# A planned kernel whose planner prices an operation by when its successor can begin

## The chip, the cores and the metric

The kernel runs on one core of one Trainium2 chip. The metric is the device time of one execution in microseconds; of several executions the median is given.

## What is computed

Three layers in a row on a batch of 4 sequences of 576 tokens, all in float32:

```
scores = q kT / 8 - slope * (i - j) where 0 <= i - j < 128      # 8 heads of 64
x      = softmax(scores) v                                      # (4, 576, 512)
u      = x + (relu(xT w_tok1) w_tok2)T                          # mixes tokens, hidden 256
u      = u + relu(u w_ch1) w_ch2                                # hidden 1536
out    = u + relu(norm(u) w1) w2                                # hidden 2048, norm with g_ln
```

The weights come in float64 and are brought to float32 on the chip.

## The kernel before

**Tiles.** The 2304 tokens are 18 tiles of 128. Every matmul operand of the three layers behind the attention is split into a high and a low part of the type that the fast matmul takes, and a product is three matmuls: high by high, low by high, high by low. The sums stay in float32 in `u`, one tile of 128x512 for each of the 18.

**Attention stage (about the first 160 us).** For each tile: scores on PE (line 625, two groups of heads), a predicated copy that folds the second key tile into the first (DVE, line 660), bias, scale and row minimum in one instruction per head (DVE, line 666), the exponential with its row sum (ACT, line 675), a transpose on PE into the one PSUM buffer `ps_t` (line 682), a copy of it to SBUF (ACT, `pf`, line 384), two triangular selections on POOL (line 692), values on PE (line 637) into the one PSUM buffer `ps_v`, and a normalization: copy `ut` (ACT), transposes back (PE, line 704), multiplication into `u` (DVE, line 400). The token layer (`tok1`, lines 469 to 471, and `tok2`, lines 764 to 766) is fed in between, three pieces for each half tile (`TOK_RATE`). The weights of that layer are converted in the same stage: a DMA brings the 8-byte numbers into `rh` and `rw` (`rh` has one buffer), ACT makes `e` from `rh` (line 445), DVE makes the float32 number in four instructions (lines 448 to 460).

**Products stage (the rest).** The two channel layers go through 14 steps each for two blocks of eight tiles, and 14 narrow ones for two tiles. In a step, `seven_products` (lines 1125 to 1127) makes a hidden block of two by two parts with seven products in place of eight, ACT and DVE evacuate, and `second` (lines 1238 to 1240) multiplies by the second weight into one of two PSUM buffers `tok`, which DVE adds to `u` (line 1243). The last layer's second block uses `second_fast` (line 1275). Sums and low parts on operands in SBUF may go to DVE or to POOL (`minus`, lines 400 and 402), whichever the planner finds.

**The order.** Each engine works its instructions off in the order of the program, and waits on semaphores where an input is not there. That order comes from a planner, class `Plan`. Every operation is recorded with a cost for each engine that may do it, its reads and its writes. `ranks` gives each a due time: PE operations from the running sum of PE costs, the others later, and then backwards through what depends on them:

```python
late[d] = min(late[d], late[k] - self.lat(e, e2) - self.STRETCH * ops[d][0][e])
```

`order` then plays the program: it goes to the engine that is free first, takes the due-soonest operation that is ready there, and sets

```python
start[k], free[e] = max(at, free[e]), max(at, free[e]) + ops[k][0][e]
...
ready[j] = max(ready[j], free[e] + self.lat(e, "PE" if "PE" in ops[j][0] else "") if k in ops[j][2] else at + 1)
```

So a cost is how long the engine is taken, and a latency `LAT` comes on top of it before a reader on another or the same engine may begin (140 more where the reader is PE). The operations are then emitted in the order of `start`. The times of this play are used for nothing else. With equal times the engine whose name comes first in the alphabet is served first, DVE before POOL. An engine is held for an operation that is due earlier and ready within `HOLD` (200 for DVE and ACT, 300 for POOL).

The costs stand in the functions `dve`, `act`, `pool_tt`, `pool_ts` and `pe` (lines 313 to 334) and as plain numbers at some calls of `op`.

Of the kernel before, what the change touches and what calls it, by code (L numbers as in the profile page):

```python
# [35 lines left out]
HW = CW // 2  # L36
# [84 lines left out]
class Plan:  # L121
# [13 lines left out]
    SPARE = {"DVE": 1200, "ACT": 0}  # L135
    LAT = {"PE": 400, "DVE": 260, "ACT": 290, "POOL": 180, "DMA": 4000, "CTL": 0}

# [175 lines left out]
def dve(n, fast=False):  # L313
    return 150 + n / (1.92 if fast else 0.97)


def act(n, psum=False, pointers=0):
    return 170 + (0.82 if psum else 0.9) * n + 93 * pointers


def pool_tt(n):
    return 150 + 2.4 * n

# [5 lines left out]
def pe(n):  # L329
    return 2.6 + n / 2.4  # L330


def pe2(n):
    return 13 + n / 2.4


def block_kernel(tc, qT, kT, v, wt1, wt2, wa1, wa2, wb1, wb2, g, bias, out):
# [72 lines left out]
    def load_f64(src, k, n, dst=None, get=None):  # L410

        rh = buf("raw", [P, DM, 4], I16, "rh", 1)
        rw = buf("raw", [P, DM, 2], U32, "rw", 2)
        e = buf("cvt", [P, DM], BF16, "e", 1)
        s = buf("cvt", [P, DM], BF16, "s", 1)
        m = buf("cvt", [P, DM], U32, "m", 1)  # L420
        at = k * P * n * 8
        flat = src.bitcast(U8).rearrange("r b -> (r b)")

        def rows(x, first):
            return x.rearrange("p n t -> p (n t)"), flat[first:first + P * n * 8].rearrange("(p b) -> p b", p=P)
# [12 lines left out]
        load_half(rw, at + 3)  # L438

        def half(x):  # L440
            return x.t[:, :n].bitcast(I32)

        op({"ACT": act(n)}, lambda: nc.scalar.activation(  # L445
            out=e.t[:, :n], in_=head(BF16), func=AF.Copy, scale=2.0 ** -116), [rh], [e])

        op({"DVE": 1.3 * dve(n // 2, True)}, lambda: nc.vector.tensor_scalar(
            half(s), half(e), 3, EXP16, ALU.logical_shift_left, ALU.bitwise_and), [e], [s])
        op({"DVE": 1.3 * dve(n // 2)}, lambda: nc.vector.scalar_tensor_tensor(  # L450
            out=half(s), in0=half(e), scalar=SIGN16, in1=half(s), op0=ALU.bitwise_and, op1=ALU.bitwise_or), [e], [s])
        op({"DVE": 1.3 * dve(n, True)}, lambda: nc.vector.tensor_scalar(
            m.t[:, :n], rw.t[:, :n, 0], 4, None, ALU.logical_shift_left), [rw], [m])
# [6 lines left out]
        op({"DVE": 1.3 * dve(n)}, lambda: nc.vector.scalar_tensor_tensor(  # L460
            out=get(), in0=m.t[:, :n], scalar=2.0 ** 32, in1=s.t[:, :n], op0=ALU.add, op1=ALU.mult), [m, s], [dst])
        return dst, get
# [144 lines left out]
    def packed(i, i2):  # L607
# [21 lines left out]
        if i2 is not None:  # L629
            tiles2 = keys_of(i2)[0]  # L630
            na = len(tiles2)
            for c in range(2):
                def values(c=c, pf=pf_t[i2, c]):
                    for p in range(2):
                        for a, kt in enumerate((i2, i2 - 1)[:na]):
                            for j in range(2):
                                nc.tensor.matmul(pv.t[j * D:(j + 1) * D, 2 * c + p], vs[kt].t[:, 4 * c + 2 * p + j],  # L637
                                                 pf.t[:, a, 2 * p + j], start=(a == 0), stop=(a == na - 1))

                parts.append((na * 440, values, [(pf_t[i2, c], a) for a in range(na)] + [vs[kt] for kt in tiles2],  # L640
                              [(pv, c)]))
# [10 lines left out]
    def softmax(i, c):  # L652
# [5 lines left out]
        if na == 2:  # L658
            b = slice((1 - own) * P, (2 - own) * P)
            op({"DVE": 690}, lambda: nc.vector.copy_predicated(  # L660
                ps.t[:, :, :, o], after.t.bitcast(I32).unsqueeze(1).unsqueeze(1).to_broadcast([P, 2, 2, P]),
# [3 lines left out]
        for m in range(4):  # L665
            op({"DVE": 358}, lambda m=m: nc.vector.tensor_tensor_reduce(  # L666
                out=t.t[:, m], in0=ps.t[:, m % 2, m // 2, o], in1=bias_sb.t[:, table, 4 * c + m],
# [6 lines left out]
        for m in range(4):  # L674
            op({"ACT": 580}, lambda m=m: nc.scalar.activation(  # L675
                out=pr.t[:, m], in_=t.t[:, m], func=AF.Exp, bias=mn.t[:, m:m + 1], scale=-1.0,
# [6 lines left out]

        op({"PE": 400}, transposes, [pr, ident], [pt])

# [3 lines left out]
        else:  # L689
            copy((pf, 1), lambda: pf.t[:, 1], pt, lambda: pt.t, 4 * P, ("ACT",), True)  # L690
            for a in range(2):
                op({"POOL": 630}, lambda a=a: nc.gpsimd.affine_select(  # L692
                    pf.t[:, a], pf.t[:, 1], [[0, 4], [1 - 2 * a, P]], (ALU.is_ge, ALU.is_gt)[a], 0.0,
                    base=0, channel_multiplier=2 * a - 1), [(pf, 1)], [(pf, a)])

    def normalize(i):
# [8 lines left out]

        op({"PE": 400}, transposes, [ut, ident], [pv])
        rc = buf("small", [P, H, 1], F32, "rc", 2)
# [152 lines left out]
    def turned(layer, places):  # L860
# [6 lines left out]
        if layer == 1:  # L867
            x = buf("mlp", [P, 4, P], F32, "st", ST_BUFS)
            for j, (i, k) in enumerate(places):
                op({"ACT": 330}, lambda i=i, j=j, g=get[j]: nc.scalar.activation(  # L870
                    out=x.t[:, j], in_=g(), func=AF.Identity, bias=nmr.t[:, i:i + 1], scale=rstd.t[:, i:i + 1]),
                    [u[i], (nmr, i), (rstd, i)], [(x, j)])
# [6 lines left out]

        op({"PE": 430}, emit, [*xs, ident], [b])  # L880
        return b
# [366 lines left out]
    def second_fast(s, w2, hid):  # L1248
# [17 lines left out]
        def product(group, x, h, w, start, stop):  # L1266
# [10 lines left out]

            op({"PE": 6 * pe2(HW)}, emit, [hh, hl, wh, wl], [o])

# [201 lines left out]
```

## Time and profile before

| | |
|---|---|
| median of 3 runs | 834.79 us |
| lowest, highest | 834.41, 836.09 us |
| profiled execution, its own time | 835.71 us |
| span of the profiled execution | 834.0 us |
| mean granted TensorE clock | 1.000 |
| PE, PEld, DVE, ACT, POOL busy, share of the span | 98%, 83%, 79%, 52%, 56% |

The span runs from the first to the last instruction; 1.7 us of the execution's time lie around it. A PE instruction's end is modelled, and matmuls overlap, so that "busy" for PE only tells where it had nothing at all in hand; the distance from one start to the next tells the rate.

### The profile page before, as it was taken

The page shows a single profiled execution, that of the slowest core. Times are in us where ns is not written, and L with a number is a line of the kernel's source. Part 1 is how long each engine was busy: PE and PEld are TensorE (multiplying, and loading weights), DVE is VectorE, ACT ScalarE, POOL GpSimd, SP SyncE. Part 2 cuts the span into 40 slices and gives each one's busy share as a digit, 9 for nine tenths or more (in the row PEclk, how much of TensorE's full clock was granted, in tenths as well). Part 3 has the DMA queues.
Part 4 walks back from the last instruction along what each step waited for, and adds up shares of the span by engine and source line. Part 5 has one row for each costly group of instructions (what it writes and reads, how often), then busy time and mean ns, then how long its engine had stood idle before and what let it go on. Part 6 is the DMA issues. An engine that isn't in the chain of part 4 may idle for free.

```text
span 834.0 us, 14315 instructions
## 1 busy us (share of the span) xinstructions
PE 820.6 (98%) x4732; PEld 691.7 (83%) x4732; DVE 658.4 (79%) x1372; ACT 430.8 (52%) x1015; POOL 466.4 (56%) x708
## 2 busy tenths in 40 slices
PE   8998999999999999999999999999999999999998
PEld 6777788888888898888888888888889889999996
DVE  5786878978898989978889868989666767777785
ACT  6887777633344535234368333447456634444440
POOL 2685366755454667543338666857533656666650
PEclk9999999999999999999999999999999999999999
DMA  8679657443678799977861544888977663443202
GB/s 301 194 215 275 227 173 224 134 158 111 232 252 283 272 335 334 348 266 266 269 238 55 186 158 137 296 306 299 356 250 243 219 226 136 131 141 122 103 26 101
DMA packets 79898, 179.20 MB, mean 215 GB/s; under 512 B 9040, under 2 KB 9168, under 8 KB 79824
## 3 DMA queue, kind: packets, MB, share of 16 engines
q1 hardware_dynamic: 79344, 176.98, 63.3%
q0 software_dynamic: 480, 1.31, 0.6%
q8 instruction: 37, 0.61, 0.3%
q14 instruction: 37, 0.30, 0.1%
HBM read 138.15 MB, written 38.80 MB: 212 GB/s over the span
## 4 chain that ended last, share of the span: by engine, by line
PE 90%; DVE 3%; DMA 3%; ACT 1%; POOL 1%; issue 1%; SPq 0%; ACTq 0%; DVEq 0%; POOLq 0%
PE tok L1238 11%; PE tok L1240 11%; PE tok L1239 10%; PE b L1125 10%; PE b L1126 10%; PE b L1127 10%; PE tok L1275 5%; PE p L1275 4%; PE ps_v L637 3%; PE ps_s L625 2%; PE p L878 2%; PE b L471 2%; PE b L470 2%; PE b L469 2%; PE tok L766 1%; PE tok L764 1%
## 5 line engine op out<-in xcount | busy, mean ns | idle before, releaser
L1243 DVE TENSOR_TENSOR u<-tok,u 128x512 f32<-128x512 f32 x196 | 133.8, 685 | 47.8 <-PE tok L1240 46.1
L1238 PE MATMUL tok<-w2h,hh 128*128 128x512 f32 x392 | 154.2, 393 | 0.2 <-DVE u L1243 0.2
L1240 PE MATMUL tok<-w2h,hl 128*128 128x512 f32 x392 | 153.0, 390 | 0.2 <-DVE hl L958 0.2
L1239 PE MATMUL tok<-w2l,hh 128*128 128x512 f32 x392 | 152.9, 390 | 0.0
L1125 PE MATMUL b<-xh,w1h 128*128 128x512 f32 x384 | 150.4, 392 | 0.0
L1126 PE MATMUL b<-xl,w1h 128*128 128x512 f32 x384 | 149.8, 390 | 0.0
L1127 PE MATMUL b<-xh,w1l 128*128 128x512 f32 x384 | 149.5, 389 | 0.0
L402 POOL TENSOR_TENSOR w1l<-w,w1h 128x256 fp32r<-128x256 f32 (+1 forms) x110 | 77.4, 725 | 103.5 <-ACT w1h L384 99.0
L956 ACT ACTIVATE hh<-b 128x512 fp32r<-128x512 f32 (+1 forms) x112 | 58.7, 542 | 147.1 <-PE b L1127 104.1
L958 DVE SCALAR_TENSOR_TENSOR hl<-b,hh 128x512 fp32r<-128x512 f32 (+1 forms) x112 | 67.4, 617 | 26.3 <-ACT hh L956 25.7
L1240 PEld LDWEIGHTS tok<-w2h,hl 128*128 128x128 f32 x392 | 73.6, 188 | 16.4 <-DVE hl L958 0.8
L1238 PEld LDWEIGHTS tok<-w2h,hh 128*128 128x128 f32 x392 | 73.7, 188 | 15.5 <-DVE u L1243 1.3
L402 POOL TENSOR_TENSOR w1l<-st,w1h 128x256 fp32r<-128x256 f32 x70 | 55.3, 811 | 55.5 <-ACT w1h L384 49.7
L1239 PEld LDWEIGHTS tok<-w2l,hh 128*128 128x128 f32 x392 | 73.7, 188 | 14.3
L1127 PEld LDWEIGHTS b<-xh,w1l 128*128 128x128 f32 x384 | 72.1, 188 | 15.4
L1125 PEld LDWEIGHTS b<-xh,w1h 128*128 128x128 f32 x384 | 72.3, 188 | 13.9 <-DVE b L400 0.2
L1126 PEld LDWEIGHTS b<-xl,w1h 128*128 128x128 f32 x384 | 72.2, 188 | 13.5
L445 ACT ACTIVATE e<-rh 128x512 bf16<-128x512 bf16 (+2 forms) x65 | 41.5, 639 | 62.1 <-DMA rh<-wb 35.6
L675 ACT ACTIVATE pr<-t,mn 128x128 f32<-128x128 f32 x144 | 55.9, 392 | 13.7 <-DVE mn L666 13.7
L692 POOL TENSOR_SCALAR_AFFINE_SELECT pf<-pf 128x512 f32<-128x512 f32 x64 | 42.5, 663 | 30.1 <-ACT pf L384 27.9
L400 DVE TENSOR_TENSOR b<-b,p 128x512 f32<-128x512 f32 x56 | 38.9, 694 | 19.8 <-PE b L1127 18.7
L402 POOL TENSOR_TENSOR st<-w 128x128 f32<-128x128 f32 x68 | 37.3, 573 | 24.1 <-PE tok L1240 5.5
(188 smaller groups left out, 1909.7 us busy)
## 6 DMA issues: line engine op xcount, KB each, us to landing
w<-d SPq DMA_DIRECT2D x86, 256.0 KB, 4.1
rw<-wb SPq DMA_DIRECT2D x32, 512.0 KB, 5.3
rh<-wb SPq DMA_DIRECT2D x32, 512.0 KB, 5.3
rw<-wa SPq DMA_DIRECT2D x24, 512.0 KB, 4.5
rh<-wa SPq DMA_DIRECT2D x24, 512.0 KB, 4.4
d<-y SPq DMA_DIRECT2D x30, 256.0 KB, 5.0
keys<-kT SPq DMA_DIRECT2D x18, 256.0 KB, 4.3
q<-qT SPq DMA_DIRECT2D x18, 256.0 KB, 4.5
```

The lines of the kernel that those rows point to most:

```text
L402: ENGINE[e].tensor_tensor(get()[:, c], ga()[:, c], gb()[:, c], alu)
L675: op({"ACT": 580}, lambda m=m: nc.scalar.activation(out=pr.t[:, m], in_=t.t[:, m], func=AF.Exp, bias=mn.t[:, m:m + 1], scale=-1.0, accum_o ...
L956: op({"ACT": act(n, True)}, lambda: nc.scalar.activation(out=hh.t[:, c], in_=go(), func=AF.Relu), [o], [(hh, key)])
L958: mark[0] = op({"DVE": dve(n)}, lambda: nc.vector.scalar_tensor_tensor(out=hl.t[:, c], in0=go(), scalar=0.0, in1=hh.t[:, c].bitcast(F32), ...
L1125: nc.tensor.matmul(g.t, wh.t[:, w], xh.t, start=start and k == 0, stop=False, skip_group_check=True)
L1126: nc.tensor.matmul(g.t, wh.t[:, w], xl.t, start=False, stop=False, skip_group_check=True)
L1127: nc.tensor.matmul(g.t, wl.t[:, w], xh.t, start=False, stop=stop and k == 1, skip_group_check=True)
L1238: nc.tensor.matmul(o.t, hh.t[:, c:c + P], wh.t, start=j == 0, stop=False)
L1239: nc.tensor.matmul(o.t, hh.t[:, c:c + P], wl.t, start=False, stop=False)
L1240: nc.tensor.matmul(o.t, hl.t[:, c:c + P], wh.t, start=False, stop=j == 1)
L1243: op({"DVE": dve(DM)}, lambda o=o, i=i: nc.vector.tensor_tensor(u[i].t, o.t, u[i].t, ALU.add), [o], [u[i]])
L1275: nc.tensor.matmul(o.t[:, p], x()[:, c], y(), start=start and p == 0 and k == 0, stop=stop and p == 1 and k == 2, skip_group_check=True)
```

## The change

The planner's costs become the time until the next instruction on the engine can begin, and the latencies grow by about what the costs lose, so that the time until a reader can begin stays about where it was for most operations. PE's cost for a matmul of n columns becomes 13 + n/2.4 everywhere (it was that in one place, `pe2`, and 2.6 + n/2.4 elsewhere). Nothing else in the program is touched: the same instructions on the same data, except where the planner now puts an operation with a choice of engines on the other one, and their order on each engine.

```diff
-    LAT = {"PE": 400, "DVE": 260, "ACT": 290, "POOL": 180, "DMA": 4000, "CTL": 0}
+    LAT = {"PE": 400, "DVE": 340, "ACT": 400, "POOL": 230, "DMA": 4000, "CTL": 0}
 def dve(n, fast=False):
-    return 150 + n / (1.92 if fast else 0.97)
+    return 70 + n / (1.92 if fast else 0.97)
 def act(n, psum=False, pointers=0):
-    return 170 + (0.82 if psum else 0.9) * n + 93 * pointers
+    return 60 + (0.82 if psum else 0.9) * n + 93 * pointers
 def pool_tt(n):
-    return 150 + 2.4 * n
+    return 130 + 2.25 * n
 def pe(n):
-    return 2.6 + n / 2.4
-def pe2(n):
     return 13 + n / 2.4
```

In `load_f64` the four DVE instructions go from 1.3 to 1.2 times `dve`. The plain numbers:

```
values, per group of heads and key tile (PE)   440 -> 480
copy_predicated (DVE, line 660)                690 -> 600
bias, scale and minimum (DVE, line 666)        358 -> 211
exponential (ACT, line 675)                    580 -> 385
four transposes (PE, lines 682 and 704)        400 -> 436
triangular selection (POOL, line 692)          630 -> 606
normalizing copy (ACT, line 870)               330 -> 385
four transposes (PE, line 878)                 430 -> 436
second_fast, six matmuls (PE, line 1275)       pe2 -> pe, the same number
```

## Rows read from the trace of the kernel before

**Rows 1.** The page, busy time of the engines.
```profile
PE 820.6 (98%) x4732; PEld 691.7 (83%) x4732; DVE 658.4 (79%) x1372; ACT 430.8 (52%) x1015; POOL 466.4 (56%) x708
```

**Rows 2.** Busy time by stretch: length, then each engine's us, PEclk, DMA share, GB/s.
```profile
0.00:20.00 20.00, 15.86 (x124) 12.87 (x124) 10.66 (x62) 14.26 (x57) 5.29 (x20) 1.00 0.86 303
...
60.00:80.00 20.00, 17.11 (x160) 13.28 (x162) 14.29 (x65) 15.99 (x63) 10.76 (x20) 1.00 0.96 273
...
160.00:834.00 674.00, 669.53 (x3439) 571.02 (x3437) 536.14 (x907) 310.62 (x606) 371.47 (x542) 1.00 0.63 212
```

**Rows 3.** Timeline of PE, products stage: start us, length us, engine, line, instruction.
```profile
231.66 0.39 PE L1125 MATMUL b<-xh,w1h 128*128 128x512 f32 x1
...
239.82 0.39 PE L1125 MATMUL b<-xh,w1h 128*128 128x512 f32 x1
```

**Rows 4.** Waits of PE's weight loads, 20 to 160 us: total, times, longest.
```profile
PEld ps_s L625 <- issue: 3.2, 12, 0.4
PEld ps_t L682 <- ACT pf L384: 2.9, 4, 1.5
...
PEld ps_v L704 <- ACT ut L384: 2.5, 4, 0.9
PEld tok L470 <- POOL xl L402: 1.8, 3, 0.7
...
PEld ps_t L682 <- ACT pr L675: 1.5, 7, 0.2
...
PEld tok L764 <- DVE u L769: 0.2, 1, 0.2
```

**Rows 5.** The same, 160 to 834 us.
```profile
PEld tok L1238 <- DVE u L1243: 1.3, 3, 0.7
PEld tok L1240 <- DVE hl L958: 0.8, 2, 0.6
```

**Rows 6.** Timeline of DVE and ACT, two instructions in a row on each.
```profile
203.01 0.69 DVE L958 SCALAR_TENSOR_TENSOR hl<-b,hh 128x512 fp32r<-128x512 f32 x1 [0.79 <-ACT hh L956]
...
203.35 0.64 ACT L384 ACTIVATE w1h<-st 128x512 fp32r<-128x512 f32 x1
...
203.62 0.47 DVE L452 TENSOR_SCALAR m<-rw 128x512 uint32<-128x512 uint32 x1
...
203.87 0.42 ACT L384 ACTIVATE w1h<-w 128x256 fp32r<-128x256 f32 x1
```

**Rows 7.** Timeline of the attention stage, 67 to 77 us.
```profile
67.86 0.39 ACT L675 ACTIVATE pr<-t,mn 128x128 f32<-128x128 f32 x1
...
68.24 0.39 ACT L675 ACTIVATE pr<-t,mn 128x128 f32<-128x128 f32 x1
...
70.97 0.28 DVE L666 CUSTOM_DVE_ANT_0 t<-ps_s,bias_sb 128x128 f32<-128x128 f32 x1
...
71.18 0.29 DVE L666 CUSTOM_DVE_ANT_0 t<-ps_s,bias_sb 128x128 f32<-128x128 f32 x1
...
72.45 0.46 ACT L445 ACTIVATE e<-rh 128x288 bf16<-128x288 bf16 x1 [3.73 <-DMA rh<-wt]
...
73.45 0.71 PE L682 MATMUL ps_t<-ident,pr 128*128 128x128 f32 x4 [1.24 <-ACT pf L384]
...
75.81 0.50 PE L766 MATMUL tok<-hh,fewl 128*128 128x512 f32 x1 [0.58 <-POOL fewl L402]
```

**Rows 8.** Groups by line and shape, 0 to 160 us: busy us, mean ns, idle before.
```profile
L675 ACT ACTIVATE pr<-t,mn 128x128 f32<-128x128 f32 x144 | 55.9, 392 | 13.7 <-DVE mn L666 13.7
...
L666 DVE CUSTOM_DVE_ANT_0 t<-ps_s,bias_sb 128x128 f32<-128x128 f32 x144 | 32.1, 285 | 5.4 <-PE ps_s L625 5.3
```

**Rows 9.** Groups by line and shape of DVE, 160 to 834 us.
```profile
L1243 DVE TENSOR_TENSOR u<-tok,u 128x512 f32<-128x512 f32 x196 | 133.8, 685 | 47.8 <-PE tok L1240 46.1
...
L452 DVE TENSOR_SCALAR m<-rw 128x512 uint32<-128x512 uint32 x45 | 26.4, 586 | 0.1
...
L400 DVE TENSOR_TENSOR w1l<-st,w1h 128x512 fp32r<-128x512 f32 x17 | 16.8, 986 | 0.0
```

More of the change, by code (lines that the diff above doesn't have):

```diff
@@ L446, in load_f64 @@
             out=e.t[:, :n], in_=head(BF16), func=AF.Copy, scale=2.0 ** -116), [rh], [e])
-        op({"DVE": 1.3 * dve(n // 2, True)}, lambda: nc.vector.tensor_scalar(
+        op({"DVE": 1.2 * dve(n // 2, True)}, lambda: nc.vector.tensor_scalar(
             half(s), half(e), 3, EXP16, ALU.logical_shift_left, ALU.bitwise_and), [e], [s])
-        op({"DVE": 1.3 * dve(n // 2)}, lambda: nc.vector.scalar_tensor_tensor(
+        op({"DVE": 1.2 * dve(n // 2)}, lambda: nc.vector.scalar_tensor_tensor(
             out=half(s), in0=half(e), scalar=SIGN16, in1=half(s), op0=ALU.bitwise_and, op1=ALU.bitwise_or), [e], [s])
-        op({"DVE": 1.3 * dve(n, True)}, lambda: nc.vector.tensor_scalar(
+        op({"DVE": 1.2 * dve(n, True)}, lambda: nc.vector.tensor_scalar(
             m.t[:, :n], rw.t[:, :n, 0], 4, None, ALU.logical_shift_left), [rw], [m])
@@ L458, in get @@
                 return y.t[:, :n]
-        op({"DVE": 1.3 * dve(n)}, lambda: nc.vector.scalar_tensor_tensor(
+        op({"DVE": 1.2 * dve(n)}, lambda: nc.vector.scalar_tensor_tensor(
             out=get(), in0=m.t[:, :n], scalar=2.0 ** 32, in1=s.t[:, :n], op0=ALU.add, op1=ALU.mult), [m, s], [dst])
@@ L638, in values @@
                                                  pf.t[:, a, 2 * p + j], start=(a == 0), stop=(a == na - 1))
-                parts.append((na * 440, values, [(pf_t[i2, c], a) for a in range(na)] + [vs[kt] for kt in tiles2],
+                parts.append((na * 480, values, [(pf_t[i2, c], a) for a in range(na)] + [vs[kt] for kt in tiles2],
                               [(pv, c)]))
@@ L659, in softmax @@
             b = slice((1 - own) * P, (2 - own) * P)
-            op({"DVE": 690}, lambda: nc.vector.copy_predicated(
+            op({"DVE": 600}, lambda: nc.vector.copy_predicated(
                 ps.t[:, :, :, o], after.t.bitcast(I32).unsqueeze(1).unsqueeze(1).to_broadcast([P, 2, 2, P]),
@@ L665, in softmax @@
         for m in range(4):
-            op({"DVE": 358}, lambda m=m: nc.vector.tensor_tensor_reduce(
+            op({"DVE": 211}, lambda m=m: nc.vector.tensor_tensor_reduce(
                 out=t.t[:, m], in0=ps.t[:, m % 2, m // 2, o], in1=bias_sb.t[:, table, 4 * c + m],
@@ L674, in softmax @@
         for m in range(4):
-            op({"ACT": 580}, lambda m=m: nc.scalar.activation(
+            op({"ACT": 385}, lambda m=m: nc.scalar.activation(
                 out=pr.t[:, m], in_=t.t[:, m], func=AF.Exp, bias=mn.t[:, m:m + 1], scale=-1.0,
@@ L682, in transposes @@
                 nc.tensor.transpose(pt.t[:, m], pr.t[:, m], ident.t)
-        op({"PE": 400}, transposes, [pr, ident], [pt])
+        op({"PE": 436}, transposes, [pr, ident], [pt])
         pf = pf_t[i, c] = buf("atb", [P, 2, 4, P], F32, "pf", PF_BUFS)
@@ L691, in softmax @@
             for a in range(2):
-                op({"POOL": 630}, lambda a=a: nc.gpsimd.affine_select(
+                op({"POOL": 606}, lambda a=a: nc.gpsimd.affine_select(
                     pf.t[:, a], pf.t[:, 1], [[0, 4], [1 - 2 * a, P]], (ALU.is_ge, ALU.is_gt)[a], 0.0,
@@ L704, in transposes @@
                 nc.tensor.transpose(pv.t[:, p], ut.t[:, p], ident.t)
-        op({"PE": 400}, transposes, [ut, ident], [pv])
+        op({"PE": 436}, transposes, [ut, ident], [pv])
         rc = buf("small", [P, H, 1], F32, "rc", 2)
@@ L869, in turned @@
             for j, (i, k) in enumerate(places):
-                op({"ACT": 330}, lambda i=i, j=j, g=get[j]: nc.scalar.activation(
+                op({"ACT": 385}, lambda i=i, j=j, g=get[j]: nc.scalar.activation(
                     out=x.t[:, j], in_=g(), func=AF.Identity, bias=nmr.t[:, i:i + 1], scale=rstd.t[:, i:i + 1]),
@@ L878, in emit @@
                 nc.tensor.transpose(b.t[:, j * P:(j + 1) * P], g(), ident.t)
-        op({"PE": 430}, emit, [*xs, ident], [b])
+        op({"PE": 436}, emit, [*xs, ident], [b])
         return b
@@ L1276, in emit @@
                                          stop=stop and p == 1 and k == 2, skip_group_check=True)
-            op({"PE": 6 * pe2(HW)}, emit, [hh, hl, wh, wl], [o])
+            op({"PE": 6 * pe(HW)}, emit, [hh, hl, wh, wl], [o])
         def fork(group):
```

## The prediction

> **What bounds the kernel now.** I read the page first: PE has work in hand 98% of the span, the next engine, DVE, 79% [rows 1]. Then the stages: the busy time by stretch shows where the other 2% lie. In the first 20 us PE has nothing in hand for 4.1 us (20.00 less 15.86), from 60 to 80 us for 2.9 us, and in the 674 us from 160 us on for 4.5 us, part of which is the tail behind the last matmul [rows 2]. A busy PE may still be slow, since matmuls overlap. So next the distance from start to start on the timeline: 36 matmuls of 512 columns start between 231.66 and 239.82 us, 0.2267 us each [rows 3]. Neighbours of one product and of the next keep that distance: PE takes instructions as fast as it does anywhere in this trace, and no order of the others makes it faster there. Last the waits of PE's weight loads, which see gaps that the modelled ends hide. From 160 us on, five groups of waits sum to 3.1 us, led by `u` and `hl` that come late from DVE [rows 5]. From 20 to 160 us, 20 groups sum to 21.5 us; 7.8 us of that is in four groups put down to issue, where no other engine is late, and 13.7 us to other engines, 6.9 us of it to ACT in the three groups pf, ut and pr [rows 4]. The reader is to see that an order can give back time almost only in the attention stage, at most 13.7 us behind its start, and that the products stage has 3.1 us to gain and 670 us in which something can be lost.
>
> The Trainium skill, Perfetto Trace Analysis, section Identifying the Most-Contended Engine, proposes another measure of the room: TensorE's distance to its best is told by the busy share of weight loads and not by that of matmuls. By that, 83% [rows 1] would leave 17%, some 140 us of the span; here a stage almost without gaps has nearly the same share, 571.02 of 674.00 us or 85% [rows 2], while the starts follow one another at 0.2267 us. I take the sum of waits.
>
> **The change, part by part.** No instruction is added or removed, so no operation costs anything by itself. What changes is the order, and where operations with a choice of engine go.
>
> 1. Are the new costs nearer to the chip? PE: 13 + 512/2.4 is 226 ns, and the trace has 226.7 [rows 3]; the old 216 was 5% short. DVE: a low part of 512 elements starts at 203.01 us and its successor at 203.62, 0.61 us; the new cost is 598 ns, the old 678. ACT: a copy of 512 starts at 203.35 us and its successor at 203.87, 0.52 us; new 521, old 631 [rows 6]. The exponential: starts 67.86 and 68.24 us, 0.38 us; new 385, old 580. Bias and minimum: 70.97 and 71.18 us, 0.21 us; new 211, old 358 [rows 7]. So yes, for instructions that run undisturbed.
>
> 2. What the latencies keep. A DVE operation of 512: 678 + 260 before, 598 + 340 after, 938 both. An ACT copy of 512: 631 + 290 and 521 + 400, 921 both. For single operations the reader's ready time does not move; only what queues behind them moves up. Four exponentials and the transposes behind them: 4 x 580 + 290 + 140 = 2750 before, 4 x 385 + 400 + 140 = 2080 after. That is the largest single shift, 0.67 us in each of 36 half tiles.
>
> 3. The attention stage. The old plan charges ACT 144 x 580 = 83.5 us for exponentials alone, which take 144 x 0.38 = 54.7 us on the chip, and DVE 144 x 358 = 51.6 us for what takes 144 x 0.21 = 30.2 us [rows 7, 8]. With the copies pf, ut and xh at about 600 each (72 x 0.6 = 43 us) the old plan holds ACT for at least 127 us, besides the weight conversions, in a stage of some 160 us. It therefore plans around an ACT that is nearly as full as PE; the chip's ACT is not, since it is busy 14.26 and 15.99 us in two of these 20 us stretches [rows 2]. With the new costs ACT needs 144 x 0.385 + 72 x 0.49 = 91 us for the same, and PE is the only full engine in the plan, as on the chip. What PE waits for ACT there should shrink. From below the gain is nothing (the waits hang on one-buffer PSUM rings that no price changes), from above it is all 13.7 us [rows 4]. The nearest rows are the three ACT groups; one of them holds 1.24 us that came from a blocked queue and not from a price [rows 7]. I take half of the 6.9 us: 3.5 us.
>
> 4. The products stage. The new costs leave out that DVE and POOL slow each other. The low part of a weight from two SBUF operands takes DVE 986 ns where the addition from PSUM of the same size takes 685, and the shift of 512 words 586 ns where the old plan charged 541 and the new charges 404 [rows 9]. The old plan paid for this with its 80 ns too much per operation; the new one has no such margin. So some evacuations by DVE should come later than planned. One late evacuation costs PE 2.1/5 = 0.42 us (1.3 and 0.8 us in 3 and 2 waits [rows 5]). From below: 3.1 us gained if all waits go. From above: one late evacuation more in each of the 28 wide steps, 28 x 0.42 = 11.8 us. The rows of the densest kind lie near the low end: five such waits in the whole stage, with DVE busy 80% of it (536.14 of 674.00 [rows 2]). I take two more, 0.8 us lost.
>
> 5. PE's own cost. With 226 for 216, 5% more of PE's time passes in the plan for each matmul, and the due times of all else spread by as much. I cost that at nothing: all engines' due times stretch alike, and it moves the plan toward the chip. If the cover is gone it shows as late evacuations, in part 4.
>
> The sum: 835.71 us of the profiled execution, less 3.5, plus 0.8, is 833.0 us. That execution lies 0.92 us above the median of the runs, 834.79; against the median the forecast is 832.1 us.
>
> **The rivals.**
>
> A. Waits change places. The transposes and the copy `pf` share the one `ps_t` buffer, and `ut` and the normalization the one `ps_v`; whatever the order, PE must come back to each. For it: the 7.8 us of issue and the short mean waits (1.5 us in 7 [rows 4]). Against it: the old ACT price is off by 50%, and its waits are the larger ones. Time: 834.8 us.
>
> B. DVE comes late in the products stage, and the kernel is slower. With the new prices DVE is idle more often in the plan, gets the tie against POOL, and takes more of the low parts that either may do; there each costs 986 ns for a planned 598. It blocks what stands behind it in the queue, the additions `u` and low parts `hl`, for which PE's two `tok` buffers and the hidden parts wait. For it: rows 5 and 9 name these very waits. Against it: with DVE at 80%, only five of them occur now. It decides against the change from (3.5 + 1.7)/0.42, about 12 late evacuations more. Three in every four wide steps, 21, give 21 x 0.42 = 8.8 us: 834.8 - 3.5 + 8.8 = 840.1 us. The Trainium skill, SBUF — State Buffer, section SBUF: two separate sides, makes this sharper: GpSimd and a VectorE instruction with two SBUF inputs exclude each other for a whole instruction of the one that came first. The 301 ns between the two rows agree with a part of such a block on average. By that rule each operation that moves to DVE is the risky kind, and the case would be this one.
>
> C. The attention stage runs ahead of its transfers. ACT stood 3.73 us for `rh` of a token weight, and PE then 1.24 and 0.58 us for what was queued behind [rows 7]; the plan counts a transfer's latency as 4000 as before. If the softmax is planned tighter, two more such blocks would cost 2 x 1.82 = 3.6 us and leave nothing of the gain: 834.8 + 3.6 = 838.4 us. Against it: PE's planned time grows as well, which gives the transfers more time.
>
> D. The whole attention stage falls in line: 13.7 us less, and half of it is already much: 834.8 less 7 to 13.7 is 821.1 to 827.8 us, say 827 us. For it: the old price of ACT binds that stage in the plan. Against it: seven of the waits, those for `pr`, are 0.2 us at most [rows 4], about the distance of two matmuls, too little for an order to aim at.
>
> **How the numbers follow.** Two runs of this kernel can't be told apart within 0.2%, 1.7 us. The forecast (a gain of 1.7 to 6 us, 828.8 to 833.1) has 0.40, A 0.20, B 0.24, C 0.08, D 0.08. Faster: forecast and D, 0.48. Same: A, 0.20. Slower: B and C, 0.32. The predicted time is 832.1 us. The range must take in C and the greater part of B on one side, and the edge of D on the other: 827.5 to 840.0 us leaves out most of D and the upper part of B, some 2 in 10.
>
> **What would show it.** Right: from 20 to 160 us the weight loads' waits for pf, ut and pr fall from 6.9 us to about 3.5; the first product matmul starts earlier; from 160 us on the waits stay under 4 us; starts stay at 0.2267 us. Part 4 or B is seen in the waits `tok` for `u` and `hl` by DVE, in more low parts (line 400) on DVE and fewer on POOL (line 402), and in their mean time. C is seen as a wait of ACT for `rh` in the attention stage. The prediction is wrong if the products stage loses more than 3.5 us, or if the attention stage's waits only change names.

## The result and the profile after

The kernel became slower: a median of 846.17 us (843.46 to 847.22 in four runs) beside 834.6 us for the kernel before in the same measurement, a ratio of 1.012 with a 95% interval of 1.010 to 1.0141. The prediction was 832.1 us with a range of 827.5 to 840.0 us. The profiled execution took 847.22 us with a span of 845.2 us, 11.2 us above the 834.0 us before. In the changed kernel all lines behind the cost functions stand four lower: the addition to `u` is line 1239 for 1243, the hidden block's first product 1121 for 1125.

The page's busy times of the kernel after, which answer to [rows 1]:

```profile
PE 825.2 (98%) x4732; PEld 692.8 (82%) x4732; DVE 678.5 (80%) x1407; ACT 428.9 (51%) x1015; POOL 423.3 (50%) x637
```

The work is the same, but some of it has moved: DVE has 35 instructions more and POOL 71 fewer, about two for one, since POOL does an operation as two halves. Of the 365 operations with a choice, DVE had 122 and now has 157.

Busy time by stretch, after (the columns of [rows 2]), with the stage's stretches first and four of two microseconds near the start behind them:

```profile
0.00:20.00 20.00, 15.66 (x97) 12.63 (x98) 7.77 (x51) 9.66 (x39) 3.71 (x17) 0.83 0.82 285
60.00:80.00 20.00, 17.74 (x174) 13.95 (x174) 15.15 (x59) 14.09 (x51) 14.05 (x26) 1.00 1.00 292
160.00:845.00 685.00, 675.00 (x3454) 572.28 (x3452) 559.87 (x947) 312.56 (x611) 331.87 (x476) 1.00 0.61 209
12.00:14.00 2.00, 0.73 (x4) 0.72 (x4) 0.43 (x5) 2.00 (x10) 0.00 (x0) 0.71 1.04 406
14.00:16.00 2.00, 2.00 (x10) 1.43 (x10) 0.00 (x0) 1.55 (x6) 0.87 (x2) 0.50 1.05 397
16.00:18.00 2.00, 2.00 (x10) 1.12 (x8) 0.89 (x3) 0.00 (x0) 0.64 (x1) 0.50 0.84 271
18.00:20.00 2.00, 2.00 (x19) 1.74 (x18) 1.85 (x12) 0.04 (x1) 0.00 (x0) 0.58 0.45 91
```

Two things stand out. From 160 us on PE has nothing in hand for 10.0 us (685.00 less 675.00) where it was 4.5 us [rows 2]. And in the first 20 us the granted clock, the column before the DMA share, is 0.83 where it was 1.00. Yet where nothing is late, PE runs as it did [rows 3], 39 matmuls in 8.84 us, 0.2267 us each. Two rows of its timeline after:

```profile
230.70 0.39 PE L1121 MATMUL b<-xh,w1h 128*128 128x512 f32 x1
...
239.54 0.39 PE L1121 MATMUL b<-xh,w1h 128*128 128x512 f32 x1
```

**Where the 11.2 us are.** I went through PE's starts in the trace's records of both kernels: each instruction has a usual distance to the next (taken as 0.2263 us for a matmul of 512 columns, 0.1197 for 256, and so on), and whatever a start is later than that, by more than 0.03 us, is a gap. The rest of the span is then the same 806 us in both, so the gaps account for all of the difference: 28.0 us before, 39.2 after. By stage: 4.97 to 7.70 us in the first 20 us, 18.35 to 18.11 from 20 to 160 us, 4.71 to 13.41 behind that. So 8.7 us were lost in the products stage, 2.7 at the start, and the attention stage behind its start gave back 0.24. By other choices of what is usual the 8.7 us stay between 8.0 and 8.8, while the other two shift by one to two microseconds, since the short matmuls of the attention have no one distance. So it isn't settled whether the attention stage gained or lost. The same sums for each experiment are in the table behind them.

**The products stage.** Waits of PE's weight loads after, 160 to 846 us (total, times, longest), which answer to [rows 5]:

```profile
PEld tok L1234 <- DVE u L1239: 4.9, 7, 1.6
PEld tok L1236 <- DVE hl L954: 2.7, 2, 1.4
PEld b L1121 <- ACT b L380: 1.9, 2, 1.5
PEld b L1121 <- DVE b L396: 1.2, 3, 0.6
PEld tok L1271 <- ACT w1h L380: 0.9, 1, 0.9
PEld b L1121 <- DVE hl L954: 0.7, 2, 0.5
PEld b L1121 <- issue: 0.2, 1, 0.2
```

Seven groups sum to 12.5 us where five summed to 3.1. The same two lead, `u` and `hl` by DVE in front of `tok`: nine waits of 7.6 us, 0.84 us each, for five of 0.42. One of them in the timeline, DVE and then PE from 578 us:

```profile
578.69 0.32 DVE L444 TENSOR_SCALAR s<-e 128x256 int32<-128x256 int32 x1
578.94 0.68 DVE L448 TENSOR_SCALAR m<-rw 128x512 uint32<-128x512 uint32 x1
579.54 0.68 DVE L446 SCALAR_TENSOR_TENSOR s<-e,s 128x256 int32<-128x256 int32 x1
580.14 0.95 DVE L396 TENSOR_TENSOR w2l<-w,w2h 128x512 fp32r<-128x512 f32 x1
581.01 0.94 DVE L456 SCALAR_TENSOR_TENSOR y<-m,s 128x512 f32<-128x512 uint32 x1
581.88 1.28 DVE L954 SCALAR_TENSOR_TENSOR hl<-b,hh 128x512 fp32r<-128x512 f32 x2
...
581.94 0.39 PE L1235 MATMUL tok<-w2l,hh 128*128 128x512 f32 x1
583.21 0.50 PE L1236 MATMUL tok<-w2h,hl 128*128 128x512 f32 x1 [0.88 <-DVE hl L954]
```

PE stands 0.88 us for a low part `hl`, and DVE is not idle for a moment: five instructions that prepare a weight stand ahead of it in the queue. They take 3.19 us from the first start (578.69) to that of `hl` (581.88). The new costs charge them 244 + 404 + 401 + 598 + 717 = 2364 ns; the old ones charged 368 + 542 + 538 + 678 + 881 = 3007. The new charge is 0.83 us short here, the old one would be 0.18 us short. The longest gap follows at once: the matmul at 587.68 us starts 1.37 us late, for an addition to `u` behind five such instructions, which take 3.87 us from 583.08 us on and are charged 2004 ns (2462 by the old costs). Eight of the ten gaps of more than 0.3 us in this stage are ended by DVE, and ahead of each DVE has worked without a pause for two microseconds or more.

A charge that is short isn't enough for a long wait, though. DVE in the kernel before, from 572 us:

```profile
572.38 1.02 DVE L400 TENSOR_TENSOR w1l<-w,w1h 128x256 fp32r<-128x256 f32 x1
573.32 1.22 DVE L460 SCALAR_TENSOR_TENSOR y<-m,s 128x512 f32<-128x512 uint32 x1
574.47 0.96 DVE L400 TENSOR_TENSOR st<-st,w 128x256 f32<-128x256 f32 x1
575.35 0.96 DVE L452 TENSOR_SCALAR m<-rw 128x512 uint32<-128x512 uint32 x1
576.22 0.68 DVE L1243 TENSOR_TENSOR u<-tok,u 128x512 f32<-128x512 f32 x1
```

Here four instructions of weight preparation take 3.84 us ahead of an addition to `u`. The old costs charge them 414 + 881 + 414 + 542 = 2251 ns, 1.59 us too little, and yet PE's next start, at 576.96 us, is only 0.39 us late. Both plans put weight preparation ahead of evacuations and charge it too little; what the wait costs depends on when PE needs the evacuation.

**The start.** PE's timeline of the kernel before, and then of the kernel after:

```profile
11.07 0.66 PE L682 MATMUL ps_t<-ident,pr 128*128 128x128 f32 x4 [0.69 <-ACT pf L384]
11.65 2.00 PE L625 MATMUL ps_s<-keys,q 64*128 64x256 f32 x16
13.58 1.09 PE L637 MATMUL ps_v<-pf,v 128*64 128x128 f32 x16
```

```profile
11.25 0.66 PE L678 MATMUL ps_t<-ident,pr 128*128 128x128 f32 x4 [0.69 <-ACT pf L380]
13.27 1.12 PE L678 MATMUL ps_t<-ident,pr 128*128 128x128 f32 x4 [1.35 <-ACT pf L380]
14.31 3.79 PE L621 MATMUL ps_s<-keys,q 64*128 64x256 f32 x16
18.03 1.88 PE L633 MATMUL ps_v<-pf,v 128*64 128x128 f32 x16
```

Before, the next scores stood between two groups of transposes and covered the copy `pf`. After, the transposes follow one another, and PE waits 1.35 us for that copy. In that wait the granted clock falls to 0.50, the lower level of 1.2 GHz, and by the rows of windows it is there for some 6.8 us (two microseconds at half show 0.50, so a shortfall of 0.29 is 1.2 us of them; with the 4 us at 0.50 and 1.7 us of the last two, 6.8). Sixteen score matmuls take 3.79 us for 2.00, sixteen for the values 1.88 for 1.09: 2.6 us. Of the four executions, the one whose mean granted clock was 1.000 took 843.46 us, the others, at 0.996 and 0.997, 846.15 to 847.22.

The three groups of the attention stage that part 3 rested on, waits of the weight loads from 20 to 160 us [rows 4], after:

```profile
PEld ps_v L700 <- ACT ut L380: 3.3, 4, 2.0
...
PEld ps_t L678 <- ACT pf L380: 1.7, 1, 1.7
...
PEld ps_t L678 <- ACT pr L671: 1.6, 6, 0.5
```

They sum to 6.6 us for 6.9.

### The profile page after: what moved, and what is told of

It reads as the page before. It is cut to its first block, busy times and chain, and to the rows that moved or that the text cites. A ratio compares the mean times of both kernels' runs of the same rounds, so it can differ in the third digit from the quotient of the medians.

```text
span 845.2 us, 14233 instructions
## 1 busy us (share of the span) xinstructions
PE 825.2 (98%) x4732; PEld 692.8 (82%) x4732; DVE 678.5 (80%) x1407; ACT 428.9 (51%) x1015; POOL 423.3 (50%) x637
## 4 chain that ended last, share of the span: by engine, by line
PE 60%; DVE 6%; POOL 4%; issue 2%; ACT 2%; DMA 1%; SPq 0%; POOLq 0%; DVEq 0%; ACTq 0%
PE tok L1234 8%; PE b L1121 8%; PE b L1122 8%; PE tok L1235 8%; PE tok L1236 8%; PE b L1123 8%; PE tok L1271 5%; PE p L1271 3%; POOL fewh L398 2%; DVE st L396 2%; PE b L465 1%; PE b L467 1%; PE b L466 1%; DVE u L1239 1%; POOL w1l L398 1%
## 5 line engine op out<-in xcount | busy, mean ns | idle before, releaser
L398 POOL TENSOR_TENSOR w1l<-w,w1h 128x256 fp32r<-128x256 f32 (+1 forms) x100 | 72.9, 750 | 119.9 <-ACT w1h L380 114.0
L954 DVE SCALAR_TENSOR_TENSOR hl<-b,hh 128x512 fp32r<-128x512 f32 (+1 forms) x112 | 67.0, 615 | 20.9 <-ACT hh L952 20.4
L1122 PEld LDWEIGHTS b<-xl,w1h 128*128 128x128 f32 x384 | 72.2, 188 | 13.1
L398 POOL TENSOR_TENSOR w1l<-st,w1h 128x256 fp32r<-128x256 f32 x46 | 38.1, 850 | 64.9 <-ACT w1h L380 54.2
L380 ACT ACTIVATE w1h<-w 128x256 fp32r<-128x256 f32 (+1 forms) x83 | 46.0, 556 | 6.8 <-PE b L1122 5.1
```

What stands on the lines that cost most here:

```text
L398: ENGINE[e].tensor_tensor(get()[:, c], ga()[:, c], gb()[:, c], alu)
L954: mark[0] = op({"DVE": dve(n)}, lambda: nc.vector.scalar_tensor_tensor(out=hl.t[:, c], in0=go(), scalar=0.0, in1=hh.t[:, c].bitcast(F32), ...
L1122: nc.tensor.matmul(g.t, wh.t[:, w], xl.t, start=False, stop=False, skip_group_check=True)
```

## The theories and the experiments

Five theories, above all for the products stage. **T1, moved work:** 35 operations more on DVE make its evacuations late (rival B). **T2, margin:** what DVE was overcharged kept its evacuations ahead of background work, and true prices per instruction leave out what contention costs. **T3, a fitted order:** the old plan is one lucky order among many, and any change of price loses. **T4, PE's margin:** with 226 for 216 ns due times spread, and work that is due becomes late. **T5, ACT's price.**

**First: engines or order, a nudge, PE alone.** The first kernel has all the new prices, but each of the 365 operations stays on the engine that it had before; the second has the old prices, with the engines of the kernel after.

```diff
+PIN = "PPDDPPPPPDPP..."   # one letter for each operation with a choice
...
+        if len(cost) > 1:
+            self.pin[k] = {"D": "DVE", "P": "POOL"}[PIN[len(self.pin)]]
...
-                for e in op[0]:
+                for e in ([self.pin[k]] if k in self.pin else op[0]):
```

> The changed kernel's prices and order, but each of the 365 operations that DVE or POOL may do stays on the engine it has in the kernel before (122 on DVE; the changed kernel has 157). Theory 1, moved work: the loss in the products stage (waits of PE that sum to 8.7 us more than before) comes from the 35 more operations on DVE, so it falls below 3 us, and the time is about 840 us (834.6 plus 2.7 us of the slower clock at the start plus 2 to 3). Theory 2, no margin: the order itself is made with too cheap a DVE, so the loss stays at 6 us or more, and the time is 843 to 847 us. Theory 3, any other order loses: also 840 to 847 us, with waits in other places than the changed kernel's.

> The prices of the kernel before, but the 365 operations with a choice go where the changed kernel has them (157 on DVE for 122). Theory 1, moved work: the products stage loses 6 us or more, and the time is 840 us or above, with no slower clock at the start. Theory 2, no margin: with the old prices' margin the order copes with the moved work, the loss is under 2 us, 834 to 837 us. Theory 3: 837 to 842 us.

The first took 843.55 us, 1.0097; the second 837.07 us, 1.0025. Waits of the weight loads from 160 us on, engines of after under the old prices:

```profile
PEld p L1284 <- DVE hl L409: 1.3, 3, 0.4
PEld tok L1249 <- DVE hl L967: 1.1, 2, 0.7
PEld b L1136 <- DVE w1l L409: 0.6, 1, 0.6
PEld b L1134 <- ACT b L393: 0.4, 1, 0.4
```

That is 3.4 us with 157 operations on DVE. T1 falls: the moved work is no burden in the old order, and most of the loss (6.8 of 8.7 us) stays when the work doesn't move.

> The kernel before with ACT's price 1 ns higher (171 for 170), which says nothing new of the chip; 46 of the 365 operations with a choice change engine, 116 on DVE for 122, and 104 of 858 PE operations change place. Theories 1 and 2: the same within 0.3%, 833 to 837 us, since DVE has no more work and the same margin. Theory 3, the order before is a lucky one and any other loses: 838 us or more.

```diff
 def act(n, psum=False, pointers=0):
-    return 170 + (0.82 if psum else 0.9) * n + 93 * pointers
+    return 171 + (0.82 if psum else 0.9) * n + 93 * pointers
```

One nanosecond on ACT's price cost 0.45% (839.13 us), with 3.2 us more of gaps in the products stage. That speaks for T3, as far as it goes, and it is the measure for what follows: a change of that size can come from any new order.

> The kernel before with PE's new prices alone (13 + n/2.4 for every matmul, 436 and 480 for the plain numbers); DVE, ACT and POOL as before; DVE gets 135 of the 365 operations for 122. Theory 1: a third of the moved work, so some 3 us of loss, 836 to 839 us. Theory 2: DVE keeps its margin, PE is priced right, so no loss, 832 to 835 us. Theory 3: 838 us or more.

The kernel before with `pe` at 13 + n/2.4 and PE's plain numbers new: 839.39 us, 1.0049, and 3.3 us more of gaps in the products stage, no more than the nudge of ACT.

**Second: the attention's numbers, the functions, DVE back, contended prices.** The first of these has only the attention's four numbers new; the next only `dve`, `act`, `pool_tt`, the latencies, the factor 1.2 and 385 for the normalizing copy; the third is the kernel after with DVE's price, latency and factor old; the fourth the kernel after with the prices of contended instructions. The first, third and fourth, shortened:

```diff
-            op({"DVE": 690}, ...
+            op({"DVE": 600}, ...
-            op({"DVE": 358}, ...
+            op({"DVE": 211}, ...
-            op({"ACT": 580}, ...
+            op({"ACT": 385}, ...
-                op({"POOL": 630}, ...
+                op({"POOL": 606}, ...
```

```diff
 def dve(n, fast=False):
-    return 70 + n / (1.92 if fast else 0.97)
+    return 150 + n / (1.92 if fast else 0.97)
...
-        op({"DVE": 1.2 * dve(n)}, ...      # and the three others of load_f64
+        op({"DVE": 1.3 * dve(n)}, ...
```

```diff
 def pool_tt(n):
-    return 130 + 2.25 * n
+    return 130 + 2.45 * n
...
-        cost = {"DVE": dve(n), "POOL": 2 * pool_tt(n // 2)}
+        cost = {"DVE": dve(n) + (190 * n / 512 if len(on) > 1 else 0), "POOL": 2 * pool_tt(n // 2)}
...
-        op({"DVE": 1.2 * dve(n)}, ...      # and the three others of load_f64
+        op({"DVE": 1.45 * dve(n)}, ...
```

> The kernel before with the new prices of four attention operations alone (predicated copy 600, minimum 211, exponential 385, selection 606); all prices of the products stage and the latencies are the old ones. Theory 2, no margin: the products stage keeps its margin, its gaps between PE's starts stay within 2 us of the 4.7 of before; the start may lose what the changed kernel loses there, 834 to 838 us. Theory 3, any other order loses: the products stage loses 3 us or more, as for the nudge (8.0 us of gaps), though none of its prices moved, 838 us or more. If the exponential's price was what held the attention stage back, the gaps from 20 to 160 us fall from 18.4 us to about 15.

> The kernel before with the new functions for DVE, ACT and POOL, the new latencies, 1.2 for 1.3 in the weight conversion and 385 for 330, but PE's prices and the attention's plain numbers as before. Theory 2: this holds the whole loss of margin, so the products stage has 11 us of gaps or more, 841 to 847 us. Theory 3: a draw like the others, 7 to 9 us of gaps, 837 to 841 us. Theory 1 has fallen with the second run.

> The changed kernel with DVE's own price put back: 150 + n/0.97, latency 260, 1.3 in the weight conversion; PE, ACT, POOL and the attention's plain numbers stay new. Theory 2: the margin on DVE is back, the products stage's gaps fall from 13.4 us to 7 or less, 837 to 841 us with the slower clock at the start. Theory 3: 8 to 13 us of gaps, 840 to 846 us.

> The changed kernel with the prices that the trace shows where DVE and POOL disturb each other: 190 ns more for a DVE operation of 512 on two SBUF operands, 1.45 for 1.2 in the weight conversion, 51 ns more for each POOL half of 256. Theory 2, the new prices lack contention: the products stage's gaps fall from 13.4 to 7 us or less, 837 to 841 us. Theory 3: better prices do not help, 8 to 13 us of gaps, 840 to 846 us.

The attention's numbers alone: 835.59 us, 1.0006; the gaps from 20 to 160 us fall from 18.35 to 15.78 us, and 2.2 us more at the start, where the granted clock fell to half as after, take that back. The functions alone: 1.0074, with 10.4 us of gaps in the products stage, a little under the 11 that T2 named. DVE's old price in the kernel after: 850.06 us, 1.0172, worse still, though some 4 of its 16.6 us are one event: a gap of 2.4 us at 209 us, behind which nine matmuls of 512 columns take 3.72 us for 2.04, at a granted clock of 0.50 from 210 to 212 us. Its two leading waits of the weight loads are again `u` (4.8 us in 5) and `hl` (3.0 us in 3) by DVE, now with the old price. That is the strongest evidence against a simple T2. Contended prices: 841.31 us, 1.0067, with 12.4 us in the products stage for 13.4: one microsecond less, when T2 asked for 7 or less; the rest of its advantage lies ahead of 160 us.

**Third: the attention late, PE back, two nudges.** The first sets the attention's numbers only from the fifth tile on (`385 if i > 3 else 580`, and so on), so that the start keeps its order; the second is the kernel after with PE's old costs; then `151` for `150` in `dve` of the kernel before, and `13.1` for `13` in `pe` of the kernel after.

```diff
-            op({"ACT": 580}, ...                      # and the three others
+            op({"ACT": 385 if i > 3 else 580}, ...
```

```diff
 def pe(n):
-    return 13 + n / 2.4
+    return 2.6 + n / 2.4               # and 440, 400, 400, 430 again
```

> The kernel before with the new prices of the four attention operations from the fifth tile on, so that the order of the first 35 us or so stays that of before. If the exponential's price held the attention stage back, as the prediction has it, the gaps from 20 to 160 us fall from 18.4 to about 15.8 us as in the run with the attention's prices alone, the start keeps its 5.0 us and its full clock, the products stage stays near 4.9 us, and the time is 831 to 833 us, faster than before. If every new order draws its gaps anew, the three stages sum to more than 28 us and the time is 834 us or more.

> The changed kernel with PE's old prices (2.6 + n/2.4, 440, 400, 430): a PE that the plan takes for 5% faster than it is. Theory 4, PE's price was the margin: with PE too fast in the plan, evacuations stand early in DVE's queue, so the products stage's gaps fall from 13.4 to 6 us or less, 836 to 840 us. Theory 3, every other order is a draw: 8 to 13 us of gaps, 840 to 846 us.

> The kernel before with DVE's price 1 ns higher (151 for 150). It says nothing new of the chip; 20 operations with a choice change engine and 455 of 1228 places on DVE differ, 4 of 858 on PE. Theory 3, a lucky order: products gaps of 6 us or more for 4.7, 836 us or above. Otherwise 4 to 5 us and 833 to 836 us.

> The changed kernel with PE's price 0.1 ns higher (13.1 for 13). Theory 3: a new draw, products gaps anywhere from 8 to 14 us, and a start with or without the slower clock, 838 to 847 us. If the new prices by themselves make 13.4 us, it stays within 1.5 us of that, 845 to 848 us.

The attention late: 835.30 us, 0.9993 (0.9979 to 1.0007), in its profiled execution no clock at half and 16.5 us of gaps from 20 to 160. The 831 to 833 us that would have told for the exponential's price didn't come. Its profiled execution has a span of 832.0 us, the shortest of all, but over its runs it can't be told from the kernel before. PE back: 838.95 us, 1.0034; the products stage falls from 13.4 to 9.0 us, where T4 asked for 6 or less, and the number of choices on DVE from 157 to 149. A nanosecond on DVE's price cost nothing (0.9993), and 0.1 ns on PE's in the kernel after left it at 1.0121 (two runs): one nudge in two upset the order of before, and the loss of the change outlives the one nudge that was tried on it.

**Fourth: one engine's price at a time.** Only ACT's, only POOL's, only DVE's in the kernel before, each with its own latency; and ACT's old price in the kernel after.

```diff
-    LAT = {"PE": 400, "DVE": 260, "ACT": 290, "POOL": 180, "DMA": 4000, "CTL": 0}
+    LAT = {"PE": 400, "DVE": 340, "ACT": 290, "POOL": 180, "DMA": 4000, "CTL": 0}
 def dve(n, fast=False):
-    return 150 + n / (1.92 if fast else 0.97)
+    return 70 + n / (1.92 if fast else 0.97)
...
-        op({"DVE": 1.3 * dve(n)}, ...      # and the three others of load_f64
+        op({"DVE": 1.2 * dve(n)}, ...
```

> The kernel before with ACT's new price alone (60 for 170, latency 400 for 290, 385 for 330). Theory 5, ACT's price: ACT runs sooner in the plan than DVE can follow; products gaps of 9 us or more and additions to u that begin more than 450 ns behind their matmuls on average (341 before, 524 with all functions new), 839 us or more. Theory 2, DVE's missing margin: 4.5 to 8 us of gaps, the additions under 400 ns, 835 to 838 us.

> The kernel before with POOL's new price alone (130 + 2.25 n, latency 230). The smallest of the changes, 58 ns for a half: 4.5 to 8 us of gaps, the additions under 400 ns behind, 834 to 838 us by theories 2 and 5; by theory 3, a lucky order, anything from 4 to 9 us.

> The kernel before with DVE's new price alone (70 for 150, latency 340 for 260, 1.2 for 1.3); 174 operations with a choice go to DVE for 122. Theory 2, DVE's missing margin: 9 us of gaps or more, additions more than 450 ns behind, 839 us or more. Theory 5: 5 to 7 us of gaps, additions under 400 ns, 835 to 838 us.

> The changed kernel with ACT's price put back (170, latency 290, 330). Theory 5: products gaps fall from 13.4 to 8 us or less, 836 to 841 us. Theory 2: they stay at 11 us or more, 842 to 847 us.

DVE's price alone (the diff above) gives the whole loss: 846.22 us, 1.0126, with 12.1 us in the products stage, as T2 expected; the delay of the additions to `u`, 416 ns, stays under the 450 that it named. ACT's gives 1.0018, POOL's 1.0005, and ACT's old price in the kernel after 1.0113: T5 falls. Waits of the weight loads from 160 us on under DVE's new price alone, its longest groups:

```profile
PEld tok L1238 <- DVE u L1243: 4.1, 7, 1.0
PEld b L1125 <- DVE hl L958: 2.6, 5, 1.2
PEld tok L1240 <- DVE hl L958: 2.5, 3, 1.4
```

They lead in the kernel after too: `u` and `hl` that come late from DVE.

**Fifth: DVE overcharged more, and DVE's new price with what contention costs.** The first is the kernel before with 230 for 150, a latency of 180 and a factor of 1.4; the second the kernel with DVE's new price alone, and with the `190 * n / 512` and the 1.45 of above.

> The kernel before with DVE's price moved the other way: 230 for 150, latency 180 for 260, 1.4 for 1.3; 91 operations with a choice on DVE for 122. Theory 2, margin: more of it gives as few gaps in the products stage or fewer, 3 to 5.5 us, additions to u under 350 ns behind, 832 to 837 us. Theory 3, the old price is what the rest was fitted to: 7 us or more, 838 us or above.

> The kernel before with DVE's new price where it runs undisturbed, and the measured contention where it does not: 190 ns more for 512 on two SBUF operands, 1.45 in the weight conversion; PE, ACT and POOL old. Theory 2: the price is right on average, the products stage falls back from 12.1 us of gaps to 6 or less, 834 to 838 us. Theory 3: 8 to 13 us, 840 to 847 us.

Overcharged more: 838.80 us, 1.005, with 7.1 us in the products stage, so more margin is not better either, against T2; the 2.4 us more lie within what a nudge does. New price with contention: 843.51 us, 1.0104; 9.4 us for the 12.1 without it, over a third of the way back to 4.7, where T2 asked for 6 or less. That too is within what a nudge does.

**All together.** Ratio with interval, gaps by stage in us, and the mean delay of an addition to `u`, from the end of its last matmul to its start on DVE (196 additions; worked out from the trace's records). In "DVE alone" a gap of some 3 us ends at 20.00 us, on the border, and is counted behind it:

| kernel | ratio (95%) | 0 to 20 | 20 to 160 | from 160 | delay of `u`, ns |
|---|---|---|---|---|---|
| before | | 4.97 | 18.35 | 4.71 | 341 |
| after | 1.012 (1.010 to 1.0141) | 7.70 | 18.11 | 13.41 | 553 |
| new prices, old engines | 1.0097 (1.0069 to 1.0125) | 6.54 | 15.73 | 11.55 | 488 |
| old prices, new engines | 1.0025 (1.0009 to 1.004) | 5.39 | 16.47 | 5.73 | 294 |
| ACT + 1 ns | 1.0045 (1.0027 to 1.0063) | 5.21 | 19.17 | 7.95 | 337 |
| PE alone | 1.0049 (1.0034 to 1.0065) | 6.82 | 16.84 | 8.02 | 397 |
| attention alone | 1.0006 (0.9989 to 1.0023) | 7.18 | 15.78 | 4.89 | 275 |
| functions alone | 1.0074 (1.0052 to 1.0096) | 5.78 | 17.58 | 10.37 | 524 |
| after, DVE old | 1.0172 (1.0138 to 1.0207) | 6.16 | 19.98 | 16.62 | 498 |
| after, contended | 1.0067 (1.0046 to 1.0089) | 6.19 | 15.29 | 12.39 | 630 |
| attention late | 0.9993 (0.9979 to 1.0007) | 4.80 | 16.47 | 4.80 | 268 |
| after, PE old | 1.0034 (1.0022 to 1.0047) | 6.70 | 16.13 | 9.02 | 515 |
| DVE + 1 ns | 0.9993 (0.9977 to 1.0009) | 5.58 | 19.27 | 4.46 | 341 |
| after, PE + 0.1 ns | 1.0121 (1.010 to 1.0141) | 6.91 | 18.07 | 14.23 | 571 |
| ACT alone | 1.0018 (1.0006 to 1.003) | 5.75 | 17.70 | 5.05 | 357 |
| POOL alone | 1.0005 (0.9991 to 1.002) | 5.32 | 17.13 | 5.19 | 325 |
| DVE alone | 1.0126 (1.0108 to 1.0144) | 3.83 | 21.64 | 12.12 | 416 |
| after, ACT old | 1.0113 (1.0094 to 1.0132) | 6.92 | 17.14 | 13.25 | 453 |
| DVE 230 | 1.005 (1.0031 to 1.0069) | 6.03 | 18.26 | 7.08 | 285 |
| DVE alone, contended | 1.0104 (1.0085 to 1.0123) | 6.79 | 19.71 | 9.40 | 410 |

The column from 160 us on sorts the kernels: all nine with 70 for 150 in `dve` lie at 9.0 us or above, ten of the eleven others at 8.0 or below; the eleventh is the kernel after with DVE's old price. In the kernel before with DVE at 70, 150 and 230 (and the latencies and factors that belong to them) an addition to `u` starts 416, 341 and 285 ns late. The delay goes the way that T2 says; the gaps, 12.1, 4.7 and 7.1 us, do not.

What is shown: DVE's new price is enough for the loss. By itself it brings 7.4 us of gaps in the products stage, where the two nudges of the kernel before brought 3.2 and took away 0.25, and ACT's and POOL's prices by themselves 0.3 and 0.5. That it does so by a missing margin is not shown. Three forecasts of T2 failed (the old price back in the kernel after, more margin than before, the price with contention). How much of the size is the draw of an order, T3, stays open. T4 stays open as well: PE's price alone costs 3.3 us, which a nudge does too, and taken out of the change it gives 4.4 back.

## Why the prediction was wrong

**Part 1**, the prices are nearer to the chip: right for single instructions, and of no use to the order. The trace after has the same spacings (`m` 0.60 us, exponentials 0.38 us).

**Part 2**, ready times of readers stay and only what queues behind moves up: right for the two operations that it works out. It doesn't hold for the weight conversion: `y` of 512 was ready at 881 + 260 = 1141 ns and is at 717 + 340 = 1057, since the factor of 1.2 takes away more than the latency adds. The danger was in the second half. What moved up was background work on DVE, ahead of evacuations: five instructions planned for 2.36 us that take 3.19.

**Part 3**, 3.5 us less in the attention stage: not borne out: 0.24 us measured, which may as well be nothing, the groups `pf`, `ut` and `pr` fell by 0.3 us, and all groups together from 21.5 to 20.9 us. The first product matmul starts at 161.42 us for 159.02, later and not earlier, by what the start lost. The attention's numbers alone give 1.9 and 2.6 us of gaps back there, but that doesn't show the mechanism: the three groups sum to 6.5 and 8.0 us in those kernels, and the old prices with the engines of after give 1.9 us back too. Whether the exponential's price held PE up at all stays open. And the start, which the part didn't reckon with, lost 2.7.

**Part 4**, 0.8 us lost in the products stage: this is the step that failed most, with 8.7 us measured. It named the mechanism, costs without contention and a lost margin of 80 ns for each operation, and the waits, `u` and `hl`, and then took the low end because DVE was busy only 80% of the stage. That mean hid that background work fills the queue where weights are prepared: in the rows of timeline above, before and after, DVE has no idle time at all. The term was mis-sized twice: it counted seven late evacuations where the rows for `u` and `hl` have nine, and it took each at 0.42 us where those are 0.84. Waits of the products `b` and for `w1h`, 4.7 us in 8 for 0.8 in 2, it didn't count at all. The margin that it names as the reason is, as said, not shown.

**Part 5**, PE's own cost at nothing: not borne out; alone it brings 3.3 us of gaps in the products stage, as late evacuations, where that part said to look. As a nudge brings as much, the price itself isn't shown to be the reason.

**Rivals.** B ended nearest, at 840.1 us with 8.8 us in the products stage. Its waits came, `u` and `hl`; the reason that it gives for them, more low parts on DVE, doesn't hold, so that its 8.8 us beside the 8.7 measured are in part luck. More low parts did go to DVE: groups by line and shape of DVE from 160 us on, after, for [rows 9]:

```profile
L1239 DVE TENSOR_TENSOR u<-tok,u 128x512 f32<-128x512 f32 x196 | 133.8, 684 | 40.6 <-PE tok L1236 39.6
...
L396 DVE TENSOR_TENSOR w1l<-st,w1h 128x512 fp32r<-128x512 f32 x29 | 25.6, 883 | 1.4 <-ACT w1h L380 1.1
...
L448 DVE TENSOR_SCALAR m<-rw 128x512 uint32<-128x512 uint32 x45 | 23.8, 529 | 0.2
```

There are 29 where 17 were, at 883 ns for 986. By the Trainium skill, SBUF — State Buffer, section SBUF: two separate sides, these exclude GpSimd while they run, and the 199 ns over the addition from PSUM agree with a part of such a block. So do these low parts of weights one by one: in the kernel after, ten of 57 ran while POOL stood, 687 ns each, and the others take 919 (before, 11 at 685 and 25 at 953). But the same assignment under the old prices has 5.7 us of gaps in place of 13.4. When such work is queued cost more than how much of it DVE has. A came near for the attention stage alone. C did not: ACT waits 1.7 us for `rh` of a token weight after, for 3.73 us [rows 7]. D did not.

**The clock at the start** was in no step: 2.6 us from 16 score and 16 value matmuls at half clock.

**What stays open.** Why DVE's old price in the changed kernel doesn't recover anything, though DVE's new price alone makes the whole loss: the prices act together, and without the 4 us of the gap at 209 us and the half clock behind it 12.5 are left, about as many as with the new price. The other constants of the plan (`HOLD`, `SPARE`, `AHEAD`, `STRETCH`) were left at values that stood beside the old prices; whether new ones would make the new prices pay was not tried. What the plan charged was set beside the trace at three places, and not for all nine waits. No version here is shown to be faster than the kernel before.

## What to carry to other kernels

In a list order for engines that work in sequence, a price is also a priority: charging background work its undisturbed time and no more can put it in front of what the bounding engine waits for, so weigh such a change by what may be queued ahead of an evacuation and not by how well it fits one instruction. A mean busy share (80%) says nothing of the stretches in which the queue is full; look at the timeline around the few waits that there are. And measure a change of plan against nudges of it: here a nanosecond moved the time by nothing or by 0.45%, so a loss of 1.2% needs more than one order to be believed.

## What the runs showed of the hardware

A wait of 1.35 us for one copy, 13 us into the kernel and behind one of 0.69 us, was followed by half clock for some 6.8 us and 2.6 us of loss, twice the wait itself. With an order in which scores cover that copy, the clock stayed at 1.00 in the profiled execution of the kernel before. It is no sure thing either way: one execution of the kernel after keeps a mean clock of 1.000, and other executions of the kernel before show means down to 0.996. With DVE's old price in the kernel after, a wait of 2.27 us (start to start a gap of 2.4) at 209 us was followed by half clock as well, where matmuls of 512 columns start 0.43 us apart for 0.2267.

The low part of a weight, 128x512 from two operands in SBUF, takes DVE 685 ns while POOL stands, as much as an addition from PSUM, and 953 on average beside a working POOL (919 in the kernel after).
